# Full-attention layers in tiles of 64 rows by 32 columns, two banks for each sum, and a schedule by half steps

## The chip, the cores and the metric

The kernel runs on one core of a Trainium2 chip. The metric is device time in microseconds (us) for one execution. On this core TensorE (PE) does the matmuls, VectorE (DVE) and ScalarE (ACT) work on elements and read the matmul results, GpSimd (POOL) does a few element operations, and SyncE (SP) issues nearly all DMAs. Matmul results land in PSUM, of which the program uses eight banks of 128 partitions by 512 float32 columns.

## The reference

Four layers act on `x` of 2048 rows by 512 columns: `x = x + attention(layernorm(x))`, with weights A, B, A, B. Every attention has 32 heads of 16 columns:

```
qkv = x @ wqkv                       # 2048 x 1536 -> q, k, v per head
scores = q @ k.T * 16 ** -0.5
A only: scores outside 0 <= row - column < 256 are masked
p = softmax(scores)                  # over the keys
x = x + (p @ v) @ wo
```

Layers 0 and 2 (A) are windowed, layers 1 and 3 (B, "full") see all 2048 keys. The change is in the full layers.

## The kernel before

**Tiling.** A full layer goes over four blocks of 512 queries and eight groups of four heads ("quads"): 32 quads a layer, 64 in all. A quad takes 16 steps of 128 keys (`attn_full`). Scores are laid out with keys on the partitions. Float16 operands are split in high and low parts that lie in the 64 rows of each head, so a score matmul has 64 rows, 128 columns of weights (keys) and 512 queries, and two heads run in the two halves of the rows. One score tile (`s`, two banks) holds two heads, so a step has two tiles with two matmuls each (line 780). For each tile ACT computes one exponential of 128 x 1024 into a buffer `e` in SBUF (line 784; six buffers, `EB`).

**Values.** Two steps later (`flush(2)`), four float32 matmuls multiply the four heads' `e` with V (128 rows, 17 columns, the 17th a column of ones that gives the softmax denominator; line 895). Each has its own 32 columns of the array and its own 32 partitions of the bank `acc[0]`, where the 16 steps add up. The profile counts eight where the program has four, so a float32 matmul runs as two passes.

**Epilogue.** At the end of a quad DVE transposes `acc[0]` out of PSUM (line 739); the next quad's first value matmul must wait for that. Then DVE divides by the sums.

**The special step.** In most quads (58 of 64) step 4 (`JX`) is split in query halves instead of head pairs (`halves_of`). ACT takes one half (line 804). DVE takes the other (line 808) and computes its exponential by a polynomial of 16 operations (`chain`, lines 814 to 818), two after each step (`links`); its value matmuls (`part`, line 870) come at step 12 (`JV`).

**Side work.** Projections of this or the next layer run in the same PE stream: keys and queries (`project`), values (`values`), output (`wo`, `wo_part`). They are cut in tiles of 12 (or 3) products of 128 x 512 (or 128 x 256), each issued as four column tiles of 32 (line 402), in the bank `acc[1]`. One DVE operation, or two, then reads that bank. For keys and queries POOL squares the result, and a matmul with `hsum` (line 589) sums the squares per head ("squares"). Python generators hand out this work. `Side.share` gives each step what a budget allows, and `PH["free"]`, a clock kept at build time, holds the next tile back until the bank should be read. `Side.finish`, and two `while` loops that call `sd.one(True)`, issue what is left at given points without attention work between.

**Order.** PE's order is exactly the order in which the program issues (`manual_schedule`); the other engines are ordered by the scheduler. PSUM in a full layer: two banks for the two `acc`, four for two score tiles, two for a third score tile (`PH["third"]`).

## Time and profile before

| | |
|---|---|
| three runs | 2649.82, 2655.22, 2655.87 us; median 2655.22 |
| the profiled execution's own time | 2656.6 us |
| its span in the profile | 2654.8 us |
| granted PE clock | 0.996 of full speed |
| layer 0 and preparation | 0 to 446.36 us |
| layer 1 (full), first to last exponential | 446.36 to 1403.20 us |
| layer 2 (windowed) | 1403.20 to 1692.10 us |
| layer 3 (full) | 1692.10 to 2637.60 us |
| rest | 17.20 us |
| exponentials in the full layers | 1990, and 58 half steps on DVE |

The page gives PE 97% busy and ACT 88% over the span; in the two full layers ACT is busy 97%. A busy time is the union of the instructions' intervals. ACT's intervals overlap, so its busy share hides small waits, and the distance from one instruction to the next is the better reading. "PEld" are weight loads, which run beside the matmuls. "[idle before <- X]" names what an engine waited for.

### The profile page before, as it was taken

What the parts mean: (1) busy time and instruction counts of PE and PEld (TensorE: products, weight loads), DVE (VectorE), ACT (ScalarE), POOL (GpSimd) and SP (SyncE); (2) the same over time, 40 slices, a digit from 0 to 9 for tenths busy, and PEclk for the clock granted to TensorE, in tenths of its full rate; (3) what the DMA queues carried; (4) which work ended last, traced back from release to release, by engine and by line L of the source; (5) the groups of instructions that cost most, each with busy time, mean ns of one, the idle gap of its engine ahead of it and who ended that gap; (6) DMA issues with size and microseconds to landing.
All of it is one profiled execution on the core that took longest, in us unless ns stands there. A gap on an engine that the chain in (4) does not pass through costs nothing.

```text
span 2654.8 us, 65506 instructions
## 1 busy us (share of the span) xinstructions
PE 2581.0 (97%) x26897; PEld 798.5 (30%) x26897; DVE 1480.9 (56%) x2933; ACT 2342.9 (88%) x2667; POOL 588.4 (22%) x1215
## 2 busy tenths in 40 slices
PE   8999899999999999999999999999999999999998
PEld 3333344332222222222223444422222222222221
DVE  5746654446675566545416666455545553466554
ACT  5777665999999999999997787699999999999997
POOL 1889760000000000000006787000000000000000
PEclk9999999999999999999999999999999999999999
DMA  6878866133343234222425654423222234435441
GB/s 203 202 235 264 221 187 181 57 100 115 107 100 104 80 117 116 80 73 85 128 95 158 203 162 148 146 77 94 83 77 69 87 105 140 145 113 169 135 133 50
DMA packets 293199, 341.50 MB, mean 129 GB/s; under 512 B 105928, under 2 KB 199592, under 8 KB 288280
## 3 DMA queue, kind: packets, MB, share of 16 engines
q1 hardware_dynamic: 284376, 310.17, 39.0%
q0 software_dynamic: 8512, 27.04, 3.8%
q8 instruction: 213, 3.49, 0.6%
q14 instruction: 98, 0.80, 0.1%
HBM read 226.49 MB, written 96.99 MB: 122 GB/s over the span
## 4 chain that ended last, share of the span: by engine, by line
PE 85%; DVE 6%; ACT 5%; issue 2%; POOL 1%; DMA 1%; SPq 0%; ACTq 0%; DVEq 0%
PE acc L895 32%; PE s L780 21%; PE acc L402 11%; PE b L405 7%; PE acc L929 5%; ACT e L784 4%; PE b L402 3%; PE acc L870 2%; PE bs L405 2%; PE s L799 1%; DVE ch L818 1%; DVE ot L739 1%; DMA x<-in_A_x_dram 0%; DVE xh L469 0%; POOL e L921 0%
## 5 line engine op out<-in xcount | busy, mean ns | idle before, releaser
L784 ACT ACTIVATE e<-s 128x1024 f32<-128x1024 f32 (+1 forms) x2316 | 2150.9, 1065 | 150.0 <-PE s L780 133.9
L895 PE MATMUL acc<-e,vt 128*17 128x512 f32 x7728 | 1017.7, 598 | 3.8 <-DVE z L56 1.6
L780 PE MATMUL s<-qt,kt 64*128 64x512 f16 (+3 forms) x5216 | 715.2, 353 | 22.7 <-ACT e L784 13.1
L818 DVE SCALAR_TENSOR_TENSOR ch<-ch 128x512 f32<-128x512 f32 x580 | 404.8, 698 | 13.4
L780 PEld LDWEIGHTS <-kt 64*128 64x128 f16 x5216 | 185.0, 94 | 673.6 <-issue 652.3
L739 DVE STREAM_TRANSPOSE ot<-acc 128x512 f32<-128x512 f32 x128 | 91.4, 714 | 436.8 <-PE acc L895 333.9
L921 POOL TENSOR_SCALAR_AFFINE_SELECT e<-e 128x256 f32<-128x256 f32 x512 | 233.1, 463 | 65.4 <-ACT e L784 64.4
L895 PEld LDWEIGHTS acc<-e,vt 128*17 128x17 f32 x7728 | 134.6, 95 | 347.3 <-issue 304.8
L918 POOL TENSOR_SCALAR_AFFINE_SELECT e<-e 128x256 f32<-128x256 f32 x448 | 195.8, 444 | 42.2 <-ACT e L784 39.3
L929 PE MATMUL acc<-e,vt 128*17 128x384 f32 (+2 forms) x2816 | 195.8, 387 | 0.6 <-POOL e L918 0.5
L405 PE MATMUL b<-xc,w 128*128 128x512 f16 x520 | 124.6, 384 | 8.9 <-DMA xc<-xh 5.9
L808 DVE TENSOR_SCALAR ch<-s 128x1024 f32<-128x1024 f32 x58 | 71.0, 1224 | 90.9 <-PE s L799 83.0
L686 POOL TENSOR_SCALAR vt<-vt 128x16 f32<-128x16 f32 (+1 forms) x48 | 17.9, 373 | 465.9 <-DVE vt L681 458.0
L764 POOL TENSOR_TENSOR oh<-o,oh 128x512 f16<-128x512 f32 x19 | 22.1, 1163 | 444.4 <-DVE oh L763 385.3
L402 PE MATMUL acc<-wv,xc 128*32 128x256 f16 (+1 forms) x2304 | 117.2, 299 | 0.0
L402 PEld LDWEIGHTS <-xc 128*32 128x32 f16 x2688 | 76.8, 97 | 121.9 <-issue 113.5
L402 PE MATMUL acc<-xc,w 128*32 128x512 f16 x1344 | 108.5, 379 | 0.3 <-DVE m_None L618 0.3
L570 POOL TENSOR_TENSOR sq_h<-sp_h 128x512 bf16<-128x512 f16 x27 | 28.1, 1039 | 354.6 <-DVE sp_h L564 321.3
L402 PE MATMUL acc<-xc,w_h 128*32 128x512 f16 x1296 | 104.3, 379 | 1.1 <-DVE m L618 0.6
L570 POOL TENSOR_TENSOR sq<-sp 128x512 bf16<-128x512 f16 x28 | 29.1, 1040 | 342.5 <-DVE sp L564 325.3
L681 DVE COPY vt<-acc 128x256 f32<-128x256 f32 (+1 forms) x48 | 23.5, 490 | 132.3 <-PE acc L402 132.2
L405 PEld LDWEIGHTS <-w 128*128 128x128 f16 x656 | 60.1, 98 | 98.1 <-issue 34.4
(179 smaller groups left out, 2192.0 us busy)
## 6 DMA issues: line engine op xcount, KB each, us to landing
kt<-kf SPq DMA_DIRECT2D x126, 512.0 KB
xd<-x SPq DMA_DIRECT2D x96, 256.0 KB
qt<-qs SPq DMA_DIRECT2D x96, 256.0 KB
x<-xd SPq DMA_DIRECT2D x96, 256.0 KB
w<-wd SPq DMA_DIRECT2D x16, 1024.0 KB
qs<-sp SPq DMA_DIRECT2D x48, 256.0 KB
wv<-wd SPq DMA_DIRECT2D x20, 512.0 KB
x<-in_A_x_dram SPq DMA_DIRECT2D x32, 256.0 KB
```

The source lines that it names most:

```text
L402: nc.tensor.matmul(ps[g:g + 32], a[:, g:g + 32], b, start=(i == 0), stop=(i == len(pairs) - 1), skip_group_check=True)
L405: nc.tensor.matmul(ps, a, b, start=(go and i == 0), stop=(i == len(pairs) - 1))
L570: nc.gpsimd.tensor_tensor(sq, sp[:, 0], sp[:, 0], ALU.mult)
L739: nc.vector.transpose(ot.rearrange("p b r -> p (b r)"), a)
L780: nc.tensor.matmul(ps[:, h, s0:s0 + wd_], kt[R * h:R * h + R, pr, kc:kc + P], qt[R * h:R * h + R, pr, qc:qc + wd_], start=True, stop=True)
L784: LAST["ACT"] = nc.scalar.activation(e[:, :, w0:w1], ps[:, :, w0:w1], AF.Exp, scale=SCALE).ins
L808: LAST["DVE"] = nc.vector.tensor_scalar(e, ps, SCALE * LOG2E, X_MIN, op0=ALU.mult, op1=ALU.max).ins
L818: chain.append(lambda y=y, i=i, d=d: v.scalar_tensor_tensor(y, y if i else t, d, t if i < len(X_POLY) - 1 else r, op0=ALU.add, op1=ALU.mult))
L895: nc.tensor.matmul(a[32 * h:32 * h + DH + 1, :], V[l, qd // 4, j // 8][:, j % 8, 4 * (qd % 4) + h, :], es_[h // 2][:, h % 2, :], start=(j ...
L918: last = nc.gpsimd.affine_select(v, v, pattern=[[0, 2], [-1, P]], compare_op=ALU.is_gt, fill=0.0, base=0, channel_multiplier=1)
L921: last = nc.gpsimd.affine_select(v, v, pattern=[[0, 2], [1, P]], compare_op=ALU.is_ge, fill=0.0, base=0, channel_multiplier=-1)
L929: nc.tensor.matmul(a[32 * h:32 * h + DH + 1, q * P:(q + nb) * P], V[l, (4 * c + j) // 4][:, j % 4, 4 * qd + h, :], es_[h // 2][:, h % 2, s ...
```

## The change

All matmuls of the full layers become tiles of 64 rows by 32 columns; the sums and products stay the same.

- A score tile is written by eight matmuls (four groups of 32 keys, two heads) instead of two.
- A value matmul is cut in two row halves. Each half adds into its own bank: `acc[0]` holds keys 0 to 63 of all steps, `acc[1]` keys 64 to 127. The epilogue transposes both banks (lines 782 and 784 after the change) and adds them (786).
- A side product is cut in the same way into two new banks (`PH["side"]`, `sd0` and `sd1`). `joined` copies one bank to SBUF and adds the other (lines 401 and 402). For `wo` a second multiply-add takes the place of `joined`. The squares are also split and joined.
- To find the two banks, the third score tile goes: two score tiles are left, which alternate.
- The schedule goes by slots, one per score tile (two per step): the slot's scores, one unit of values (four heads, half of the 512 queries) of four slots before (`LAG`; five in the first slots of a quad), at most one side product (`Side.slot`), and one operation of the polynomial.
- The special step loses one quad (57 on DVE, 1991 exponentials on ACT).

```diff
-JX, JV = 4, 12
+JX, JV, LAG = 4, 12, 4
...
-        if PH["full"] or not PH["win"] and "pool" not in PH or l is None and PH.get("third"):
+        if PH["full"] or "pool" not in PH or l is None and PH["side"] is not None:
             ps_x.close()
-            PH["pool"] = ps_x.enter_context(tc.tile_pool(name=f"ps_x{l}", bufs=1 if PH["full"] else 2, space=bass.MemoryType.PSUM))
-            PH["third"] = PH["pool"].tile([P, 2, QC], F32, name=f"s{l}") if PH["full"] else None
+            opened = lambda name, bufs: ps_x.enter_context(tc.tile_pool(name=f"{name}{l}", bufs=bufs, space=bass.MemoryType.PSUM))
+            PH["scores"], PH["pool"] = opened("ps_s", 2), opened("ps_x", 1 if PH["full"] else 2)
+            PH["side"] = [PH["pool"].tile([P, QC], F32, name=f"sd{r}_{l}") for r in range(2)] if PH["full"] else None
...
-            return acc[1]
+            return PH["side"]
...
+    def split(ps, a, b, start, stop, t=None):
+
+        for g in range(0, P, 32) if t is None else (32 * t,):
+            for r in range(2):
+                c = slice(g, g + 32) if t is None else slice(0, 32)
+                nc.tensor.matmul(ps[r][g:g + 32, :b.shape[-1]], a[64 * r:64 * r + 64, c], b[64 * r:64 * r + 64],
+                                 start=start, stop=stop, skip_group_check=True)
+
+    def joined(ps, to):
+
+        with tc.high_priority(HEAD_START):
+            nc.vector.tensor_copy(to, ps[1])
+            LAST["DVE"] = nc.vector.tensor_tensor(to, ps[0], to, ALU.add).ins
+        return to
...
-        if PH["full"] and pend:
-            settle()
-            PH["free"] = clock[0] + 1.6
-            yield 0.1
+        if PH["full"]:
+            PH["unit"] = PH["now"]
+            if pend:
+                settle()
+                PH["free"] = clock[0] + 2.2
+                yield 0.25
+            for i, (a, b) in enumerate(pairs):
+                split(ps, a, b, i == 0, i == len(pairs) - 1)
+                spent(us)
+                if i < len(pairs) - 1:
+                    yield us
+            PH["free"], PH["unit"] = clock[0] + after + (0.6 if chain else 0.0), None
+            READ.append(0)
+            return
...
+            if PH["full"]:
+                ps = joined(ps, vp.tile([P, QC], F32, name=f"pj{n}_{t}", tag="xn", bufs=1))
...
+            if PH["full"]:
+                split(ph, hsum, sq, True, True, t)
+            else:
+                nc.tensor.matmul(ph[32 * t:32 * t + 32, :], hsum, sq, start=True, stop=True, skip_group_check=True)
+        if not PH["full"]:
+            return ph
+        r = slice(32 * min(sqs), 32 * max(sqs) + 32)
+        to = vp.tile([P, QC], F32, name=f"ps{n}", tag="oe")
+        joined([ps[r] for ps in ph], to[r])
+        return to
...
+                if PH["full"]:
+                    n0, n1 = (0, D) if h is None else (x * HH * DH, (x + 1) * HH * DH)
+                    joined([b[:, n0:n1].rearrange("p (h d) -> p h d", d=DH) for b in ps], to)
...
+                for b in ps if PH["full"] else (ps,):
+                    LAST["DVE"] = nc.vector.scalar_tensor_tensor(xs[i], b, 1.0 / (UP[2] * UP[3]), xs[i], op0=ALU.mult, op1=ALU.add).ins
...
+            if l % 2:
+                os = vp.tile([P, QC // 32, 32], F32, name=f"os{n}", tag="oe")
+                nc.vector.transpose(os.rearrange("p b r -> p (b r)"), acc[1])
+                a = acc[0]
             nc.vector.transpose(ot.rearrange("p b r -> p (b r)"), a)
+        if l % 2:
+            nc.vector.tensor_tensor(ot[:, :, :DH + 1], ot[:, :, :DH + 1], os[:, :, :DH + 1], ALU.add)
...
+    def scores(name, kt, qt, kc, pr=None, x=None):
+
+        ps = PH["scores"].tile([P, 2, QC], F32, name=f"s{name}", tag="s")
+        for p, n in ((0, slice(0, QC // 2)), (1, slice(QC // 2, QC))) if pr is None else ((pr, slice(0, QC)),):
+            m = slice(x * QC // 2, (x + 1) * QC // 2) if pr is None else n
+            for g in range(0, P, 32):
                 for h in range(2):
...
+                    nc.tensor.matmul(ps[g:g + 32, h, n], kt[R * h:R * h + R, p, kc + g:kc + g + 32], qt[R * h:R * h + R, p, m],
+                                     start=True, stop=True, skip_group_check=True)
+        spent(0.23)
+        if x == 1:
+            e = CH["tile"][:, 0:2]
+            with tc.high_priority(HEAD_START):
+                LAST["DVE"] = nc.vector.tensor_scalar(e, ps, SCALE * LOG2E, X_MIN, op0=ALU.mult, op1=ALU.max).ins
+            for h in range(2):
+                polynomial(e[:, h])
+            return e
+        e = pp.tile([P, 2, QC], F32, name=f"e{name}", tag="e", bufs=EB)
+        LAST["ACT"] = nc.scalar.activation(e, ps, AF.Exp, scale=SCALE).ins
+        return e
...
+    def attn_full(l, c, qd, kt, qt):
+
+        def unit(j, x, where):
+            def go():
+                for h in range(4):
+                    for r in range(2):
+                        e = where(h)[64 * r:64 * r + 64]
+                        o = acc[r][32 * h:32 * h + DH + 1, x * QC // 2:(x + 1) * QC // 2]
+                        nc.tensor.matmul(o, V[l, qd // 4, j // 8][64 * r:64 * r + 64, j % 8, 4 * (qd % 4) + h, :], e,
+                                         start=(j == 0 and x == 0), stop=(j == NT - 1), skip_group_check=True)
+                spent(0.43)
+            return go
+
+        special = CH["tile"] is not None
         for j in range(NT):
+            name, kc, es_ = f"{l}_{c}_{qd}_{j}", j % 8 * P, []
+            if special and j == JX:
+                for x in range(2):
+                    e = scores(f"{name}_{x}", kt[j // 8], qt, kc, x=x)
+                    u = unit(j, x, lambda h, e=e: e[:, h % 2, h // 2 * QC // 2:(h // 2 + 1) * QC // 2])
+                    if x:
+                        held[l, c, qd] = u
+                    yield None if x else u
                 continue
             for pr in range(2):
+                es_.append(scores(f"{name}_{pr}", kt[j // 8], qt, kc, pr))
+                yield unit(j, pr, lambda h, x=pr, es_=es_: es_[h // 2][:, h % 2, x * QC // 2:(x + 1) * QC // 2])
...
-        def share(self):
-
-            self.budget = min(self.budget + max((self.cost - self.spent) / max(self.steps - 3 - self.k, 1), self.least), 0.75)
-            self.lag = max(self.lag - max(0.29, self.least), -0.3) + PH["skew"]
-            PH["skew"] = 0.0
-            while self.q and clock[0] >= PH["free"] and self.budget >= MM / 2 and (self.lag < 0.25 or self.budget > 0.45):
+        def slot(self):
+
+            self.budget = min(self.budget + max((self.cost - self.spent) / max(self.steps - 3 - self.k, 1), self.least) / 2, 0.75)
+            n = 0
+            while self.q and n < 1 and clock[0] >= PH["free"] and self.budget >= MM / 2:
                 c = self.one()
                 if c is None:
                     break
                 self.budget -= abs(c)
-                self.lag += abs(c)
+                n += abs(c) > 0.05
...
+    def quad(l, t, c, qd, ops, sd):
+
+        special = CH["tile"] is not None
+        at = PH["slots"]
+        for n, new in enumerate(attn_full(l, c, qd, *ops)):
+            j, pr = divmod(n, 2)
+            if pr == 0:
+                if (l, t, c) == (3, 0, 0):
+                    sd.least = 0.28 if LOW.done else 0.5
+                    while sd.k == NT - 5 and not LOW.done:
+                        sd.one(True)
+                while (l, c, qd) == (1, 0, NQD // 2) and sd.k == NT - 5 and not LAST_UP.done:
+                    sd.one(True)
+                sd.step()
+            if new is not None:
+                fullq.append([at + n + LAG + (n < (2 * JX + 1 if special else 10)), new, None])
+            if n == 2 * NT - 1:
+                fullq[-1][2] = lambda: epilogue(l, c, qd, None)
+            if n == 2 * JV + LAG + 1 and (l, c, qd) in held:
+                assert not chain
+                fullq[0:0] = [[at + n, held.pop((l, c, qd)), None]]
+            clock[0] = max(clock[0], PH["began"] + 0.9)
+            PH["began"] = clock[0]
+            then, ends = [], []
+            while fullq and fullq[0][0] <= at + n:
+                _, f, end = fullq.pop(0)
+                then.append(f)
+                if end:
+                    ends.append(end)
+            for f in then:
+                f()
+            if len(then) < 2:
+                sd.slot()
+            for f in ends:
+                f()
+            links(1)
+        PH["slots"] += 2 * NT
```

Three places show how the instructions stand. In the names, `s1_1_2_3_0` is the score tile of layer 1, block 1, quad 2, step 3, first head pair; `e` the exponential of the same numbers; `oh` and `wo` operands of an output projection; a number of five digits only makes a name unique.

PE at the start of quad 2 of block 1 in layer 1, before: the two score tiles of step 2, the values of step 0 (which wait for DVE's transpose), a side product.

```order
L780 MATMUL s1_1_2_2_0_9718<-qt1_1_2_9295,kt1_1_2_0_9297 128x512 [waits Activation_49]
...
L780 MATMUL s1_1_2_2_1_9723<-qt1_1_2_9295,kt1_1_2_0_9297 128x512 [waits Activation_49]
...
L895 MATMUL acc0_81<-e1_1_2_0_0_9669,vt1_0_0_4382 17x512 [waits DVE_49]
...
L402 MATMUL acc1_82<-wo1_0_8974,oh1_0_3_7475 32x512
...
L780 MATMUL s1_5721<-qt1_1_2_9295,kt1_1_2_0_9297 128x512 [waits Activation_49]
...
L780 MATMUL s1_1_2_3_1_9744<-qt1_1_2_9295,kt1_1_2_0_9297 128x512 [waits Activation_49]
```

The same place after (slots 5 and 6 of the quad, and slots 8 to 11 with the special step; the first matmul of each group of eight or sixteen):

```order
L844 MATMUL s1_1_2_2_1_15140<-qt1_1_2_14130,kt1_1_2_0_14132 32x512 [waits Activation_49]
...
L921 MATMUL acc0_78<-e1_1_2_0_0_15014,vt1_0_0_4382 17x256 [waits DVE_49]
...
L395 MATMUL sd0_1_5725<-wo1_0_13385,oh1_0_3_9640 32x512
...
L844 MATMUL s1_1_2_3_0_15167<-qt1_1_2_14130,kt1_1_2_0_14132 32x512 [waits Activation_49]
...
L921 MATMUL acc0_78<-e1_1_2_0_0_15014,vt1_0_0_4382 17x256
...
L844 MATMUL s1_1_2_4_0_15213<-qt1_1_2_14130,kt1_1_2_0_14132 32x256 [waits Activation_49]
...
L844 MATMUL s1_1_2_4_1_15248<-qt1_1_2_14130,kt1_1_2_0_14132 32x256 [waits Activation_49]
...
L844 MATMUL s1_1_2_5_0_15283<-qt1_1_2_14130,kt1_1_2_0_14132 32x512 [waits Activation_49]
...
L844 MATMUL s1_1_2_5_1_15312<-qt1_1_2_14130,kt1_1_2_0_14132 32x512 [waits DVE_49]
```

A slot has one score tile, one unit of values and one side product; the unit in slot 6 is the last reader of `e1_1_2_0_0`. Of the two score tiles, slot 10 (`5_0`) takes the one that ACT read in slot 8 and slot 11 (`5_1`) the one that DVE reads.

DVE after one query projection of layer 3, before (two operations) and after (four):

```order
L564 TENSOR_SCALAR sp3_0_2_h0_0_24712<-acc1_82 128x512 [waits DMAHW4_49,DMAHW3_49,PE_49]
L565 SCALAR_TENSOR_TENSOR sp3_0_2_h0_0_24712<-acc1_82,sp3_0_2_h0_0_24712 128x512 [waits DVE_49]
```

```order
L401 COPY pj3_0_2_h0_0_43394<-sd1_3_39681 128x512 [waits PE_49]
L402 TENSOR_TENSOR pj3_0_2_h0_0_43394<-sd0_3_39680,pj3_0_2_h0_0_43394 128x512 [waits DVE_49]
L589 TENSOR_SCALAR sp3_0_2_h0_0_43397<-pj3_0_2_h0_0_43394 128x512 [waits DMAHW4_49,DMAHW3_49,DVE_49]
L590 SCALAR_TENSOR_TENSOR sp3_0_2_h0_0_43397<-pj3_0_2_h0_0_43394,sp3_0_2_h0_0_43397 128x512 [waits DVE_49]
```

The copy and the add stand ahead of the operation whose result POOL squares.

PE at the end of quad 1 of block 1 in layer 3, before: only the squares of one projection stand between the last values and the next quad's scores.

```order
L895 MATMUL acc0_81<-e3_1_1_13_1_24857,vt3_0_1_23206 17x512 x2
L589 LDWEIGHTS hsum_86 [waits DVE_49]
L589 MATMUL acc1_82<-sq3_1_1_h1_1_24899,hsum_86 32x512 [waits Pool_49]
L780 LDWEIGHTS kt3_2_0_0_24920 [waits DMAHW7_49,DMAHW0_49]
L780 MATMUL s3_2_0_0_0_24930<-qt3_2_0_24918,kt3_2_0_0_24920 128x512 [waits Activation_49]
```

After: five products of a query projection, its squares, all twelve products of a key projection and its squares stand there.

```order
L921 MATMUL acc1_79<-e3_1_1_13_1_43236,vt3_0_1_39601 17x256
L395 LDWEIGHTS w3_0_2_h0_42380
L395 MATMUL sd0_3_39680<-xc3_2_39083,w3_0_2_h0_42380 32x512
...
L395 MATMUL sd0_3_39680<-sq3_0_2_h0_0_43400,hsum_83 32x512 [waits Pool_49]
...
L395 LDWEIGHTS w3_1_1_h1_43154 [waits DMAHW2_49]
L395 MATMUL sd0_3_39680<-xc3_1_37609,w3_1_1_h1_43154 32x512 [waits DVE_49]
...
L395 MATMUL sd0_3_39680<-sq3_1_1_h1_1_43516,hsum_83 32x512 [waits Pool_49]
...
L844 LDWEIGHTS kt3_2_0_0_43528 [waits DMAHW0_49]
L844 MATMUL s3_2_0_0_0_43538<-qt3_2_0_43526,kt3_2_0_0_43528 32x512 [waits Activation_49]
```

`Side.finish` issues there what the slots had no room for.

123 lines of the change are left out of this document (38 added, 85 removed).

## The prediction

> **What bounds the kernel now.** I read the busy shares first, then the two full layers by stage, then PE's timeline in a step, then ACT's.
>
> ```profile
> PE 2581.0 (97%) x26897; PEld 798.5 (30%) x26897; DVE 1480.9 (56%) x2933; ACT 2342.9 (88%) x2667; POOL 588.4 (22%) x1215
> 446.36:1403.20 956.84, 945.58 (x9732) 241.85 (x9733) 514.25 (x949) 928.15 (x997) 55.92 (x70) 1.00 0.32 97
> 1692.10:2637.60 945.50, 935.06 (x9497) 244.49 (x9495) 504.15 (x893) 921.66 (x994) 53.73 (x62) 1.00 0.35 106
> ...
> 1289.54 1.05 PE L895 MATMUL acc<-e,vt 128*17 128x512 f32 x8
> 1290.41 0.61 PE L402 MATMUL acc<-wo,oh 128*32 128x512 f16 x8
> 1290.95 0.61 PE L780 MATMUL s<-qt,kt 64*128 64x512 f16 x4
> 1291.49 1.05 PE L895 MATMUL acc<-e,vt 128*17 128x512 f32 x8
> 1292.48 0.60 PE L780 MATMUL s<-qt,kt 64*128 64x512 f16 x4
> ...
> 1402.06 2.59 PE acc L402 x48
> ```
>
> The second and third rows are layers 1 and 3: length, then busy time (count) of PE, PEld, DVE, ACT and POOL. PE and ACT are both near full. A side product of four tiles takes 2.59/12 = 0.216 us (last row, from the chain of waits). From the starts: values 0.87 us, two side products 0.54 where two should take 0.43, scores 0.54 where two pairs should take 0.43, and values straight before scores 0.98. So each passage between the shapes 64x128 and 128x32 costs PE about 0.11 us, twice a step. A step with one side product takes 0.54 + 0.87 + 0.216 + 0.11 = 1.74 us, with two 1.95.
>
> ```profile
> 2444.08 27.61 ACT L784 ACTIVATE e<-s 128x1024 f32<-128x1024 f32 x30 [0.71 <-PE s L780]
> L784 ACT ACTIVATE e<-s x30: 1019/1186/1367, 2444.1 to 2470.3; 128x1024 f32<-128x1024 f32 x30
> ```
>
> Thirty exponentials without a wait: starts 26.2/29 = 0.904 us apart, but each lasts longer than the one before, 1.02 us at first and 1.37 at the end. Ends are therefore (27.61 - 1.02)/29 = 0.917 apart, and a score tile comes free at an end. I take 0.917 as ACT's pace, 1.83 a step: between PE's two step lengths. Over both full layers, 1902.3 us, the 1990 exponentials need 1990 x 0.917 = 1824; **ACT's ends lose only 78 us**. Whatever the change does for PE, it can win no more than this.
>
> **What PE wins.** Without changes of shape a step saves 2 x 0.11 us, 225 us over 1024 steps, all of it PE time. If eight half-height tiles run side by side as four do now, a slot (one score tile) needs 0.22 for scores, 0.44 for half a step's values and 0.216 for a side product: 0.87 us, under ACT's 0.917. No row shows eight tiles at once. The nearest are two row halves together (scores, four matmuls in 0.43) and four column groups together (side), so I take full overlap. [...] ACT then sets the pace of the full layers: 1991 x 0.917 = 1825 us plus what ACT loses. The sum is what it loses.
>
> **How much lateness ACT bears.**
>
> ```profile
> 446.36 2.83 ACT L784 ACTIVATE e<-s 128x1024 f32<-128x1024 f32 x3
> 447.41 0.39 PE L780 MATMUL s<-qt,ke 64*128 64x512 f16 x2 [0.78 <-ACT e L784]
> ...
> 2471.22 1.38 ACT L804 ACTIVATE e<-s 128x1024 f32<-128x1024 f32 x1
> 2471.32 1.23 DVE L808 TENSOR_SCALAR ch<-s 128x1024 f32<-128x1024 f32 x1 [1.54 <-PE s L799]
> 2472.01 0.40 PE L402 MATMUL acc<-xc,w_h 128*32 128x512 f16 x4
> 2472.34 0.70 PE L780 MATMUL s<-qt,kt 64*128 64x512 f16 x4
> 2472.84 3.01 ACT L784 ACTIVATE e<-s 128x1024 f32<-128x1024 f32 x3 [0.23 <-PE s L780]
> ```
>
> From ACT's end to PE's next score I take 0.05 us (446.36 + 1.02 to 447.41 is 0.03; from DVE to PE it is 0.05 in (c)); from the score to ACT's start 0.50 (2472.34 to 2472.84), 0.54 with six more starts (an estimate). With two alternating score tiles, exponential n+2 can start 0.05 + 0.54 = 0.59 after the end of n, and must start by 2 x 0.917 - 1.02 = 0.815. PE may be 0.225 us late; now, with a third tile, it may be a whole 0.917 later. Terms, each as ACT time lost:
>
> (a) *Special step, 57 x 0.69 = 39 us.* Slot 9's tile goes to DVE; slot 10 needs the tile ACT reads in slot 8. The next end is 0.05 + 0.54 + 1.02 = 1.61 after the last, 0.69 over pace. DVE's 1.23 us is over by then. Before, this step costs about as much, since PE is behind: at 2471 the end moves from 2472.60 to 2472.84 + 1.02, 0.34 over pace; at 1017 (next rows) from 1018.78 to 1019.62 + 1.02, 0.94. Bounds 35 (0.6 each) and 50 (DVE late).
>
> ```profile
> 1017.75 1.03 ACT L804 ACTIVATE e<-s 128x1024 f32<-128x1024 f32 x1
> 1019.62 2.85 ACT L784 ACTIVATE e<-s 128x1024 f32<-128x1024 f32 x3 [0.84 <-PE s L780]
> ```
>
> (b) *Six `e` buffers, 33 us.* At the start of a quad values run five slots late. Slots 6 and 8 (in the seven quads without special step 6 to 14, even) then write the `e` that the same slot's values still read. Those values end on PE 0.22 + 0.22 + 0.05 after the slot's score, plus 0.50: the exponential starts 0.99 after the score instead of 0.765, 0.22 lost. 57 x 2 + 7 x 5 = 149 times. Bounds 0 (if the buffers turn out a slot older) and 35.
>
> (c) *Epilogue, 19 us.*
>
> ```profile
> 1012.12 1.05 PE L895 MATMUL acc<-e,vt 128*17 128x512 f32 x8
> 1012.99 0.40 PE L402 MATMUL acc<-wo,oh 128*32 128x512 f16 x4
> 1013.24 0.72 DVE L739 STREAM_TRANSPOSE ot<-acc 128x512 f32<-128x512 f32 x1 [9.08 <-PE acc L895]
> 1013.88 0.65 DVE L704 SCALAR_TENSOR_TENSOR x<-acc,x 128x512 f32<-128x512 f32 x1
> 1014.01 0.62 PE L895 MATMUL acc<-e,vt 128*17 128x512 f32 x4
> ```
>
> DVE starts 0.25 after the values have streamed (1012.12 + 0.87 = 1012.99). Two transposes take 0.64 + 0.72, and PE resumes 0.05 later. The last values stand in slot 3, the first new ones in slot 5: from slot 3's score 0.67 + 0.25 + 1.36 + 0.05 = 2.33, wanted at 2 x 0.917 + 0.22 = 2.06. PE is 0.27 late, which slot 6 passes on through (b) unless slot 5 has no side product: 0.13 on average, and 0.17 more for a busy DVE. 62 x 0.3. Bounds 4 and 40.
>
> (d) *Forced runs, 37 us.* The slots take one product whatever its width, so half-width products are not finished in time. The order shows runs without scores: 42 half-width ones at the end of quad 3 and 29 in quad 4 of layer 1's first block, 31 in layer 3's first quad (12 there before), the place shown of layer 3's block 1, and two products with squares a block later.
>
> ```profile
> 1688.95 2.51 DMA qt<-qs
> 1713.37 1.31 PE acc L402 x48
> ...
> 1713.18 1.49 PE L402 MATMUL acc<-wv,xc 128*32 128x256 f16 x48
> 1714.72 0.42 DVE L681 COPY vt<-acc 128x256 f32<-128x256 f32 x1 [1.08 <-PE acc L402]
> ```
>
> A half-width product takes 1.31/12 = 0.11; the bank turns over in 0.23 (1714.49 to 1714.72) + 0.42 + 0.05, an add that I put at 0.45, + 0.05 = 1.2, once per twelve. 42: 4.6 + 3.6; 29: 3.2 + 2.4; 31: 3.4 + 2.4; each less 0.2: 19. The place shown: 17 x 0.216, twice 3.5 (next term) for squares, 1.7 for the bank (0.25 and two of 0.72), 2.5 for a `qt` that is only then loaded: 15. The last 4. Less 1.3 for the twelve before. Bounds 17 (PE's work alone) and 45.
>
> (e) *Squares, 18 us.*
>
> ```profile
> L570 POOL TENSOR_TENSOR sq_h<-sp_h 128x512 bf16<-128x512 f16 x27 | 28.1, 1039 | 354.6 <-DVE sp_h L564 321.3
> L564 DVE TENSOR_SCALAR sp_h<-acc x27: 651/692/693, 1731.4 to 2537.9; 128x512 f16<-128x512 f32 x27
> 2472.58 0.43 DVE L814 TENSOR_SCALAR ch<-ch 128x512 f32<-128x512 f32 x1
> ```
>
> From the last product: 0.42 to DVE, copy and add 0.72 each (0.69 and a gap), scaling from SBUF 0.49 (as L814), POOL 1.04, 0.1: 3.5 us, of which the copy and the add, 1.4, are new. In the order 24 squares stand three slots behind (2.75 us) and 24 four (3.67). The first wait 0.75, less 0.225, and 0.2 for a busy DVE. Behind a waiting square stand the next score and all of PE. Bounds 0 and 35.
>
> (f) *Other side tiles, 10 us, and layer ends, 1.* A `wo` bank turns over in 0.42 + 0.65 + 0.65 + 0.05 = 1.77, the next product comes two slots (1.83) on; only a busy DVE delays it. Bounds 0 and 25. DVE goes from 514 + 504 us busy in these layers to some 1290: 64 transposes and adds, 72 second multiply-adds, 137 joins of one or two operations.
>
> Sum: 1825 + 39 + 33 + 19 + 37 + 18 + 11 = 1982 for the full layers, against 1902.3: 79 us more. The windowed layers keep their work. The profiled execution took 2656.6, so 2735.6; it stands 1.4 over the median shown, and I forecast **2735 us**.
>
> **Rivals.**
>
> *PE's relief shows (faster).* If (b) vanishes, DVE is never late and the forced runs cost only PE's work, ACT loses 35 + 4 + 17 = 56 us instead of 78: 2634 us. For it: PE has 0.05 us to spare in each slot and 0.26 where no side product stands. Against it: with two tiles it may be 0.225 late and no more.
>
> *They cancel.* Losses of 70 to 86 us, 2648 to 2664.
>
> *Matmuls do not come fast enough (much slower).* A slot has 8 + 16 + 6 = 30 matmuls with 30 loads.
>
> ```profile
> 1632.00:1640.00 8.00, 7.69 (x175) 4.69 (x169) 7.48 (x22) 6.71 (x9) 6.25 (x16) 1.00 0.35 105
> ```
>
> The densest 8 us hold 175 matmuls, 46 ns each; 48 came in 1.31 us, 27 ns each. This decides from 0.917/30 = 30.6 ns. At 33 ns a slot lasts 0.99, the 2048 slots 2028, with (a), (d) and (e) 2122: 2876 us. Tiles that overlap only in part come to the same. [...]
>
> *DVE is the limit.* Sixteen polynomial operations and a projection's four fall in slots 9 to 25. If the polynomial is 1 us late at slot 29, PE waits there in 57 quads: 45 us more, 2780. Against: 1290 of 1982 us is 65%.
>
> **How the numbers follow.** Forecast 0.56, DVE limit 0.08, slow issue 0.07, cancel 0.08, faster 0.21. What can be told from no change is 0.3%, 8 us. Faster 0.21, same 0.08, slower 0.71. The low bounds of the terms together give 56 us, 2634; the high ones 230 us, 2808. The range is 2630 to 2810.
>
> **What would show it.** Right: ACT's idle time named PE; after the special slot 1.6 us between ends; exponentials of slots 6 and 8 waiting for values; the forced runs as gaps of 5 to 14 us; PE's changes of shape gone. Wrong: score groups of eight lasting over 0.25 us (then PE is the limit), or ends 0.917 apart through slots 6 and 8 and over a quad's start, with the full layers under 1900 us.

## The result and the profile after

The changed kernel takes 2902.89 us (median of four runs, 2890.60 to 2912.94), the kernel before 2653.38 in the same comparison: 1.094 times as long, 95% interval 1.089 to 1.099. The forecast was 2735 us, with a range up to 2810. The sign was right, the size was not: 79 us more were expected, 250 came. The profile shows the slowest of the four executions, 2912.94 us, so sums taken from it come out some 10 us over the median.

The page of the changed kernel, first the busy shares, then three groups of instructions (busy time, mean ns | idle time before them and what ended it), then the queue that brings the engines' instructions (packets, MB, share of the DMA engines):

```profile
PE 2612.4 (90%) x70272; PEld 1389.2 (48%) x70272; DVE 1724.5 (59%) x3342; ACT 2361.0 (81%) x2668; POOL 610.9 (21%) x1215
L855 ACT ACTIVATE e<-s 128x1024 f32<-128x1024 f32 x1991 | 1869.0, 1061 | 285.2 <-PE s L844 212.9
L595 POOL TENSOR_TENSOR sq_h<-sp_h 128x512 bf16<-128x512 f16 x27 | 39.2, 1453 | 512.9 <-DVE sp_h L589 400.1
q8 instruction: 551, 9.03, 1.3%
```

PE is at 90% where it was at 97, and ACT at 81 where it was at 88: neither is full any more. The exponentials wait 285 us, most of it for scores. The loss lies in the full layers (length, then PE, PEld, DVE, ACT, POOL busy, granted clock):

```profile
451.00:1499.00 1048.00, 949.36 (x31448) 537.11 (x31432) 617.50 (x1120) 932.31 (x998) 67.45 (x69) 0.98 0.31 91
1787.00:2894.00 1107.00, 961.64 (x31031) 538.47 (x31039) 642.76 (x1126) 937.09 (x996) 63.56 (x62) 0.97 0.31 93
```

From the first exponential to the last end they take 1047.7 and 1106.0 us, 2153.7 against 1902.3; the windowed layers changed by some 5. With the prediction's pace of 0.917 us, ACT's ends lose 134.6 + 193.8 = 328 us where 157 were expected, and lost 78 before. "Lost" is here and below the distance from one end to the next, less 0.917 us, added up.

What the change promised for PE came true. PE's timeline in the changed kernel (start, duration, tile, count):

```profile
2335.02 0.41 PE L844 MATMUL s<-qt,kt 64*32 64x512 f16 x8
2335.24 0.63 PE L921 MATMUL acc<-e,vt 64*17 64x256 f32 x16
2335.67 0.41 PE L395 MATMUL sd<-wo,ov 64*32 64x512 f16 x8
2335.88 0.41 PE L844 MATMUL s<-qt,kt 64*32 64x512 f16 x8
```

Scores to values 0.22, values to side 0.43, side to scores 0.21: eight small tiles run side by side, no passage between shapes costs anything, and a slot takes 0.86 us. But PE stands still between such slots. Its waits in the full layers of the changed kernel, down to 8.9 us (us in total, times, longest). In the first row PE is ahead and waits for ACT, which by itself costs ACT nothing:

```profile
PE s L844 <- ACT e L855: 34.7, 98, 1.0
PE sd L395 <- DVE x L763: 29.9, 29, 4.4
PE acc L921 <- issue: 28.8, 35, 2.3
PE sd L395 <- POOL sq_h L595: 28.4, 22, 3.6
PE acc L921 <- DVE ot L784: 24.6, 27, 6.2
PE sd L395 <- issue: 18.6, 19, 2.4
PE s L844 <- issue: 14.1, 19, 1.8
PE sd L395 <- DVE vt L402: 9.1, 9, 1.5
PE sd L395 <- DVE psk L402: 8.9, 7, 2.5
```

I put every late end of an exponential down to the largest cause of PE's stalls in the 2.6 us before it, and each stall to the instruction that ended some 0.1 us before PE went on; of slot 10's losses, 0.6 us each are put to the special step, so that row is in good part set by this rule. This sorting is worked out from the trace's records; no single row shows it, and where two stalls fall together it is a choice. ACT's lost time, both full layers, by cause:

| cause | ACT us lost | prediction's term |
|---|---|---|
| PE has no instructions ("issue") | 52 | none |
| second multiply-add of wo, L763 | 44 | (f): 10 with the joins |
| squares on POOL, L595 | 42 | (e): 18 |
| special step | 40 | (a): 39 |
| epilogue's transposes, L784 | 37 | (c): 19 |
| joins, L402 | 25 | in (f) |
| runs without scores, nothing else late | 24 | (d): 37 |
| PE at half clock | 23 | none |
| `e` buffers, nothing else late | 11 | (b): 33 |
| rest, most of it other DVE work | 30 | 1 |

### The profile page after: what moved, and what is told of

The parts are those of the page before. It is cut to its first block, busy times and chain, and to the rows that moved or that the text cites. A ratio compares the mean times of both kernels' runs of the same rounds, so it can differ in the third digit from the quotient of the medians.

```text
span 2910.9 us, 152756 instructions
## 1 busy us (share of the span) xinstructions
PE 2612.4 (90%) x70272; PEld 1389.2 (48%) x70272; DVE 1724.5 (59%) x3342; ACT 2361.0 (81%) x2668; POOL 610.9 (21%) x1215
## 4 chain that ended last, share of the span: by engine, by line
PE 54%; ACT 19%; DVE 16%; issue 8%; POOL 1%; DMA 1%; SPq 0%; ACTq 0%; DVEq 0%; POOLq 0%
PE acc L921 18%; ACT e L855 17%; PE s L844 11%; PE sd L395 7%; PE b L430 6%; PE acc L970 5%; PE b L427 3%; DVE ch L865 3%; PE s L826 3%; PE bs L430 2%; DVE ot L784 1%; DVE os L782 1%; DVE x L763 1%; ACT e L830 1%; DMA x<-in_A_x_dram 1%
## 5 line engine op out<-in xcount | busy, mean ns | idle before, releaser
L855 ACT ACTIVATE e<-s 128x1024 f32<-128x1024 f32 x1991 | 1869.0, 1061 | 285.2 <-PE s L844 212.9
L921 PE MATMUL acc<-e,vt 64*17 64x256 f32 x31856 | 1379.4, 383 | 57.4 <-issue 28.8
L844 PE MATMUL s<-qt,kt 64*32 64x512 f16 (+1 forms) x17008 | 949.8, 376 | 76.2 <-ACT e L855 30.0
L921 PEld LDWEIGHTS acc<-e,vt 64*17 64x17 f32 x31856 | 617.3, 94 | 243.4 <-issue 73.8
L844 PEld LDWEIGHTS <-kt 64*32 64x32 f16 x17008 | 408.7, 91 | 545.9 <-issue 410.8
L830 ACT ACTIVATE e<-s 128x1024 f32<-128x1024 f32 (+2 forms) x384 | 354.2, 970 | 100.2 <-PE s L826 85.7
L865 DVE SCALAR_TENSOR_TENSOR ch<-ch 128x512 f32<-128x512 f32 x570 | 405.8, 712 | 14.0
L395 PE MATMUL sd<-wv,xc 64*32 64x256 f16 (+1 forms) x4608 | 193.8, 301 | 16.5 <-DVE vt L402 9.1
L395 PE MATMUL sd<-xc,w_h 64*32 64x512 f16 x2592 | 157.6, 391 | 15.3 <-issue 6.1
L395 PE MATMUL sd<-xc,w 64*32 64x512 f16 x2688 | 156.3, 376 | 6.5 <-issue 6.3
L784 DVE STREAM_TRANSPOSE ot<-acc 128x512 f32<-128x512 f32 x128 | 88.8, 693 | 102.3 <-PE acc L970 102.3
L595 POOL TENSOR_TENSOR sq_h<-sp_h 128x512 bf16<-128x512 f16 x27 | 39.2, 1453 | 512.9 <-DVE sp_h L589 400.1
L763 DVE SCALAR_TENSOR_TENSOR x<-sd,x 128x512 f32<-128x512 f32 x120 | 82.6, 688 | 92.6 <-PE sd L395 86.9
L826 PE MATMUL s<-qt,kt 64*128 64x384 f16 (+2 forms) x1408 | 116.9, 275 | 16.6 <-ACT e L830 15.9
```

The source lines that it names most:

```text
L395: nc.tensor.matmul(ps[r][g:g + 32, :b.shape[-1]], a[64 * r:64 * r + 64, c], b[64 * r:64 * r + 64], start=start, stop=stop, skip_group_chec ...
L784: nc.vector.transpose(ot.rearrange("p b r -> p (b r)"), a)
L826: nc.tensor.matmul(ps[:, h, s0:s0 + wd_], kt[R * h:R * h + R, pr, kc:kc + P], qt[R * h:R * h + R, pr, qc:qc + wd_], start=True, stop=True)
L830: LAST["ACT"] = nc.scalar.activation(e[:, :, w0:w1], ps[:, :, w0:w1], AF.Exp, scale=SCALE).ins
L844: nc.tensor.matmul(ps[g:g + 32, h, n], kt[R * h:R * h + R, p, kc + g:kc + g + 32], qt[R * h:R * h + R, p, m], start=True, stop=True, skip_ ...
L855: LAST["ACT"] = nc.scalar.activation(e, ps, AF.Exp, scale=SCALE).ins
```

## Experiments

Three theories stood at the start. F (fetch): PE runs out of instructions. L (late DVE): DVE's work on the split banks stands behind other work. T (tiles): with two score tiles any lateness costs, and the third tile is what is missed.

### 1 to 3: does PE run out of instructions?

The "issue" rows are idle time in which PE waited for nothing that the profile shows. Before, they came to 0.7 us in all; now they come to 62. In PE's timeline of the changed kernel such a stall sits in the middle of one score group:

```profile
629.19 0.49 PE L395 MATMUL sd<-xc,w 64*32 64x512 f16 x8
629.47 0.39 PE L844 MATMUL s<-qt,kt 64*32 64x512 f16 x3
631.43 0.40 PE L844 MATMUL s<-qt,kt 64*32 64x512 f16 x5 [1.57 <-issue]
631.45 0.60 PE L395 MATMUL sd<-xc,w 64*32 64x512 f16 x8
```

The third and the fourth matmul belong to one group: they read and write the same tiles. The transfers of the instruction queue are 16,384 bytes each; 551 of them for PE's 140,724 records make 255 instructions per packet, and on average 256 are used between the starts of two. In the full layers more than 0.5 us pass 286 times between the start of one PE record and the next ("gaps" below). Of these gaps 66 (77 us) end 1.25 to 1.5 us after a packet has landed; in the kernel before, 4 of 270 do. If the 286 had nothing to do with packets, some 16 would fall there, an estimate from the mean spacing of packets, 4.42 us. Run 1 takes some four tenths of the full layers' transfers away (91 and 93 GB/s become 54 and 57):

```
 def load_full(l, c, qd):
+    if l not in ONCE:
+        ONCE[l] = load_first(l, c, qd)   # the old body
+    return ONCE[l]
...
-    matmul(pf[:1, :1], okay[:, 0:1], onesf)
+    matmul(pf[:1, :1], onesf, onesf)
```

> The changed kernel without the loads of K and Q in the full layers: each full layer loads the two K tiles and the Q tile of its first quad and uses them for all 32 quads, so the attention of the other quads is left out of the result; every matmul, exponential, DVE operation and instruction stays, and the flag of the range test is set. Theory F (fetch): PE runs out of instructions. One 16 KB packet of the instruction queue holds 256 of them, 128 matmuls with their loads; a slot now has 30 such pairs, so PE uses a packet in some 3.9 us (before: 12.8), and a packet that starts behind 0.5 to 2 MB of other transfers comes 1.5 to 4 us late. F expects the PE gaps over 0.5 us that end 1.25 to 1.5 us after a packet has landed (30 in layer 1 and 36 in layer 3, 41 and 36 us long together) to fall below 20, the half-speed windows of the clock from 27 to some 15, and the time from 2903 to 2790 to 2840 us. Theory L (late DVE: second reads of the split banks, joins and epilogue stand behind polynomial links) and theory T (the third score tile is missed) expect no change: 2890 to 2915.

2860.81 us, ratio 1.077 (1.074 to 1.079): 42 us less than the changed kernel. The gaps of that kind fell from 66 to 36 (38 us), and the rows of that run are:

```profile
PE s L844 <- issue: 10.2, 13, 2.7
PE acc L928 <- issue: 8.2, 11, 1.9
PE sd L395 <- issue: 4.2, 5, 1.3
```

23 us are left of 62. Fewer than 20 gaps and 2790 to 2840 us were expected, and neither came; the stretches at half clock stayed too, 23 in the full layers with the loads and without. So the mechanism is there, at about half the price expected. The control, with the same edit to the kernel before:

> The kernel before with the same loads left out in the same way (the attention of all but the first quad's K and Q is left out of the result). A packet of instructions lasts PE 12.8 us there, so F expects no change, 2645 to 2660 us; so do L and T. If it becomes faster by more than 10 us, the loads cost something by themselves, and the gain of the changed kernel without loads is not due to the instructions.

2653.14 us, ratio 0.9998 (0.9987 to 1.0008): the loads cost nothing where a packet lasts 12.8 us (median in the full layers of the kernel before: 12.82 and 13.01). Run 3 keeps the result and only makes the loads small:

```
-for v in range(len(kts), 2):
-    kt = pp.tile([P, 2, S // 2], F16, tag="kt", bufs=3)
+for v in range(len(kts), 8):
+    kt = pp.tile([P, 2, S // 8], F16, tag="kt", bufs=12)
```

> The changed kernel with K in eight pieces of 256 columns (128 KB) per quad and twelve buffers, in place of two of 1024 (512 KB) and three: the same bytes, but a piece is loaded when the piece before it in its buffer has been used, so that an instruction packet stands behind at most some 128 to 256 KB of K. F expects part of what leaving the loads out gives: 30 to 80 us, 2820 to 2873 us, and fewer than 35 of the gaps that end 1.25 to 1.5 us after a packet. L and T expect no change, 2890 to 2915.

2874.84 us, ratio 1.084 (1.081 to 1.086): 28 us less, just short of the bound named; 47 gaps (48 us) are left, more than 35. At 30 pairs of load and matmul in 0.917 us PE uses up a packet in 3.9 us (an estimate; in the full layers of the changed kernel the median from one packet's start to the next is 3.81 and 4.13), so there is little time for one that comes late: the packets ahead of the 66 gaps started 5.3 us after the one before (median; up to 8.7). The shortest time between two packets was 3.24 us; 128 pairs at 27 ns take about as long (3.45), so this is not shown to be a limit of the delivery. How far ahead packets are fetched no run settles.

### 4: what the third score tile was worth

```
-ps = PH["third"] if PH["full"] and turn["s"] % 3 == 0 else ps_s.tile(...)
+ps = ps_s.tile(...)
```

> The kernel before, with two score tiles of two banks in place of three and nothing else changed. T expects at least 100 us more than 2653: PE may be 0.225 us late with two tiles, and the values of a whole step, 0.87 us, stand between two score groups there. If PE's own work is what bounds the kernel before, whatever the number of tiles, it stays within 30 us of 2653, and the missing tile is not what the change lost.

2880.84 us, ratio 1.085 (1.083 to 1.088). One tile less, and the kernel before loses 227 us, about as much as the change lost. ACT's ends lose 303 us in place of 78: some 8 us per layer in most of the even slots, and 35 per layer in slot 10, behind the special step. The windows and the timeline of that run:

```profile
447.40:1517.80 1070.40, 991.66 (x9724) 270.83 (x9727) 514.53 (x949) 949.79 (x997) 55.89 (x70) 1.00 0.29 87
1806.30:2863.60 1057.30, 982.47 (x9499) 268.14 (x9498) 505.15 (x893) 949.25 (x994) 53.68 (x62) 1.00 0.31 94
...
1295.02 1.05 PE L895 MATMUL acc<-e,vt 128*17 128x512 f32 x8
1295.89 0.61 PE L402 MATMUL acc<-xc,w 128*32 128x512 f16 x8
1296.43 0.60 PE L780 MATMUL s<-qt,kt 64*128 64x512 f16 x4
1296.92 1.03 ACT L784 ACTIVATE e<-s 128x1024 f32<-128x1024 f32 x1 [0.46 <-PE s L780]
```

Values and side products, 1295.02 to 1296.43, stand between two score groups, 1.41 us. The third tile is what let ACT run on meanwhile; without it ACT waits 0.46 there. The change gives this tile up. At equal tiles the changed kernel is 22 us slower than this one, so the split of the tiles won nothing back as it stood; with the mends of run 11 below (2801 us) it is 80 us faster. The 227 us are the tile's price in the kernel before, where a whole step's values stand between score groups. In the changed kernel it is half a step's, and no run gave that kernel a third tile, so the price there is not measured.

### 5: is it the polynomial on DVE?

```
 nc.vector.tensor_scalar(e, ps, 0.0, 1.0, op0=ALU.mult, op1=ALU.max)
-for h in range(2):
-    polynomial(e[:, h])
```

> The changed kernel without the sixteen polynomial operations on DVE per special step; DVE still reads slot 9's score tile in one operation, but writes ones in place of the scaled scores, so half a step of each such quad is left out of the result, and the flag of the range test is set. PE's and ACT's instructions stay. DVE loses some 57 x 16 x 0.6 = 550 us of work. Theory L: PE's waits for DVE in the full layers (30 us for the second multiply-add of wo, 25 for the transposes, 22 for joins) fall by more than half, and with them half-speed windows; 2800 to 2850 us. Theories F (fetch) and T (two score tiles bear only 0.2 us of lateness, whatever the cause) without L expect at most 15 us: 2885 to 2905.

2860.78 us, ratio 1.076 (1.072 to 1.080): 42 us less, between the two theories. In layer 3 ACT's loss falls from 194 to 139 us: behind L763 from 44 to 12, behind the joins from 19 to 8. Squares and transposes stay (38 and 16). In layer 1 it rises from 135 to 143, since ACT's loss behind "issue" stalls grew from 28 to 45 there. So the polynomial holds up the multiply-adds of wo, in part the joins, and little else.

### 6 and 8: runs without scores, and later reuse of the side banks

```
-n += abs(c) > 0.05
+n += (abs(c) > 0.05) * (0.5 if abs(c) < 0.15 else 1)
```

> The changed kernel with up to two half-width side products per slot in place of one. The order then has no forced runs but one of 16 half-width products; in the changed kernel there are runs of 42, 29, 31 half-width and 17 whole products. By the prediction's term (d) the runs cost 37 us of ACT time; the ends of the exponentials behind them lose 43 us in the trace. Expected if (d) is right: 2860 to 2870 us against 2903. If the runs only move the work and the products cost the same elsewhere (a slot with two half-width products has no spare time more): 2890 to 2905.

2889.62 us, ratio 1.089 (1.086 to 1.092): 13 us less, which is not clear of the noise, as the four runs of the changed kernel alone span 22 us. At the five places the loss does go, in three of them nearly whole: 11.2, 5.3, 6.0, 16.0 and 4.1 us become 0.8, 0, 4.7, 3.4 and 0. But layer 1 as a whole went from 135 to 142 us, as ACT's loss behind "issue" stalls rose from 28 to 51; layer 3 lost 31 us less. The time lies just under the second range (2890 to 2905), far from the 2860 to 2870 expected if the term was right. So the term was about right at its places, and part of the gain went into another wait. Run 8 adds a slot before a bank is used again, also ahead of squares:

```
-PH["free"], PH["unit"] = clock[0] + after + ..., None
+PH["free"], PH["unit"] = clock[0] + after + 0.9 + ..., None
...
-    PH["free"] = clock[0] + 2.2           # ahead of squares
+    PH["free"] = clock[0] + 2.2 + 0.9
```

> The kernel of the run with two half-width products a slot, in which in addition a side bank is used again one slot (0.9 us) later than planned, and squares stand one slot later. Forced runs come back: about 70 whole products, 15 us of PE's work. Theory L: PE's waits in front of side products (30 us for the second multiply-add, 32 for the squares on POOL, 22 for joins) fall by more than half, and the half-speed windows with them; net 20 to 50 us below the run with two halves alone. Theories F and T without L: 10 to 20 us above it, by the forced runs.

2890.49 us, ratio 1.089 (1.087 to 1.091): no change, where L expected at least 20 us less. Two things lie behind this. The squares did profit: PE's waits for them fell from 17.4 us in run 6 to 12.8. But a wait for Q tiles came, which run 6 does not have and whose cause stays open:

```profile
PE s L844 <- DMA qt<-qs: 22.7, 5, 6.1
```

Behind L763, the reads that the edit was to relieve, PE still waits 27.1 us (26.1 in run 6) and ACT still loses 34. So these waits do not come from a reuse that is a slot too early. The timeline of the changed kernel, DVE and then PE at one such place, shows DVE's order:

```profile
2662.10 0.43 DVE L861 TENSOR_SCALAR ch<-ch 128x512 f32<-128x512 f32 x1
2662.56 0.69 DVE L862 SCALAR_TENSOR_TENSOR ch<-ch 128x512 f32<-128x512 f32 x1
2663.29 0.43 DVE L863 TENSOR_SCALAR ch<-ch 128x512 int32<-128x512 int32 x1
2663.63 2.86 DVE L865 SCALAR_TENSOR_TENSOR ch<-ch 128x512 f32<-128x512 f32 x4
2666.53 0.69 DVE L763 SCALAR_TENSOR_TENSOR x<-sd,x 128x512 f32<-128x512 f32 x1
2667.13 0.68 DVE L865 SCALAR_TENSOR_TENSOR ch<-ch 128x512 f32<-128x512 f32 x1
2667.73 0.68 DVE L763 SCALAR_TENSOR_TENSOR x<-sd,x 128x512 f32<-128x512 f32 x1
...
2667.27 0.58 PE L395 MATMUL sd<-wo,ov 64*32 64x512 f16 x1 [4.37 <-DVE x L763]
2668.47 0.62 PE L395 MATMUL sd<-wo,ov 64*32 64x512 f16 x7 [0.62 <-DVE x L763]
```

Seven links of the polynomial stand ahead of the first multiply-add, an eighth between the two. ACT's next exponential waited 5.81 us.

### 7: is it the width of the columns that makes a passage cost?

```
-for h in range(2):
-    nc.tensor.matmul(ps[:, h, ...], kt[R * h:R * h + R, pr, kc:kc + P], ...)
+for g in range(0, P, 32):
+    for h in range(2):
+        nc.tensor.matmul(ps[g:g + 32, h, ...], kt[R * h:R * h + R, pr, kc + g:kc + g + 32], ...)
```

> The kernel before, with three score tiles, values and side products in 128x32, and only the scores in eight tiles of 64 rows by 32 columns in place of two of 64 by 128. If the 0.11 us that PE loses at a passage between shapes is due to the change of the columns' width (128 to 32), the passages become free, PE wins up to 225 us of its own time and ACT up to its 78 us of lost time: 2590 to 2635 us. If it is due to the change of rows (64 to 128), nothing changes: 2645 to 2660. Instructions: 38 pairs per step, a packet per 6 us, so F expects few waits for instructions.

2672.51 us, ratio 1.0069 (1.0047 to 1.0091): 0.7% slower. PE's timeline of this run:

```profile
1290.71 1.05 PE L901 MATMUL acc<-e,vt 128*17 128x512 f32 x8
1291.58 0.61 PE L402 MATMUL acc<-wo,oh 128*32 128x512 f16 x8
1292.13 0.63 PE L785 MATMUL s<-qt,kt 64*32 64x512 f16 x16
1292.68 1.05 PE L901 MATMUL acc<-e,vt 128*17 128x512 f32 x8
```

0.87, 0.55, 0.55, as before, and no gain; that the time is even some 12 us over the 2645 to 2660 expected for that case stays unexplained. The shapes on both sides of a passage now have 32 columns, so the 0.11 us belong to the change of rows, 128 to 64 and back.

### 9 to 12: mending what was found, one by one

Each run adds one edit to the one before, from run 6 (2890) on. Theory A: the costs of late instructions add up. Theory B: a wait that is mended only lays another one bare.

```
+with tc.high_priority(HEAD_START):                            # 9
     for b in ps if PH["full"] else (ps,):
-        nc.vector.scalar_tensor_tensor(xs[i], b, ...)
+        LAST["DVE"] = nc.vector.scalar_tensor_tensor(xs[i], b, ...).ins
...
+bufs=12, K in pieces of S // 8                                # 10, as run 3
...
-... for a, b in TERMS], 2.2)                                  # 11
+... for a, b in TERMS], 3.1 if PH["full"] else 2.2)
...
-EB = 6, tag="qt" bufs=3, tag="sp" bufs=4                      # 12
+EB = 7, tag="qt" bufs=2, tag="sp" bufs=3
```

> The kernel with two half-width products a slot (2890 us); in addition DVE's two multiply-adds of a wo product in layer 3 are put ahead of the polynomial links that are ready at the same time (in the changed kernel up to five links of 0.7 us stand between or before them). Theory A (each late instruction costs PE its own stall, and the costs add): in layer 3 PE's stalls behind these multiply-adds, 39 us and 44 us of ACT time in the changed kernel, fall to about 12, as without the polynomial; 2850 to 2865 us. Theory B (with two score tiles any lateness costs, so one that is mended only lays another bare): less than half of it, 2870 to 2890.

2846.61 us (1.072, 1.069 to 1.075): 43 less, a little more than theory A expected. Behind the multiply-adds (now L764) ACT loses 6 us, and PE's row is:

```profile
PE sd L395 <- DVE x L764: 2.9, 7, 0.6
```

The changed kernel itself agrees. Layer 1's `wo` (line 744) has the same pair of multiply-adds, 24 in all, but with the priority that line 763 lacks, and no side product waits for one of them; for the 120 of line 763 PE waits 29 times. It is a partial control, since layer 1's tiles are longer, twelve products for three. The kernel before lacks the priority too (line 722), and with three score tiles and one read nothing in its trace waits for it.

> As the run before it, with K also in eight pieces per quad. Theory A: another 20 to 35 us less, as in the run with the eighths alone (28 us); theory B: less than 14.

2816.73 us (1.059, 1.057 to 1.062): 30 less, A.

> As the run before it, with the squares of a projection planned one slot (0.9 us) later. In the changed kernel PE's stalls behind the squares on POOL are 36 us long and cost ACT 42. Theory A: 20 to 35 us less than without; theory B: less than 10.

2800.65 us (1.054, 1.051 to 1.057): 16 less, between A and B. The squares' loss in ACT time went from 25 to 12.

> As the run before it, with seven buffers for exponentials in place of six (and for their memory two Q tiles in place of three and three buffers for split projections in place of four). Slots 6 and 8 then no longer write the buffer that the same slot's values read. Term (b) of the prediction puts this at 33 us; the ends at slots 6 and 8 lose 82 us in the changed kernel with everything that falls on them. Theory A: 25 to 40 us less than without; theory B, by which slot 6 loses what slots 4 and 5 were late by (epilogue) as soon as it does not wait itself: 5 to 20. All four mended by theory A: 2760 to 2790 us, near the 2735 that was forecast; the rest is the special step (40 us) and the epilogue.

2822.02 us (1.063, 1.060 to 1.066): 21 more, expected by neither. Slots 6 and 8 lose 24 us in place of 62, as A has it, but the full layers become only 9 us shorter (2041.1 after 2050.5): "issue" stalls rose by 16, slot 10 lost 11 more and other slots the rest, as B has it. Layer 1 starts at 472.0 in place of 445.3, which is more than the whole loss. This edit takes buffers from the layer ahead of it too; that they are the reason was not tested.

### 13 to 16: what is left

> Two half-width products a slot, wo's multiply-adds first and later squares, without the loads of K and Q after the first quad of a full layer (the attention of the other quads is left out of the result, the flag of the range test is set). To be held against the same mends with K in eighths, 2801 us. Theory F: what is left there of waits for instructions, 49 us of ACT time by the gaps that end 1.1 to 1.7 us after a packet, falls to some 20: 2765 to 2785 us. If the loads matter no more once K comes in eighths: 2793 to 2808.

With the edits of runs 6, 9 and 11 and that of run 1: 2786.63 us (1.050, 1.048 to 1.052), 14 below the 2801 with K in eighths, where 16 to 36 were expected. With the loads gone "issue" still costs ACT 41 us: other transfers, or PE catching up faster than packets come; which of them was not tried.

Run 14 undoes the halving of the values in the changed kernel:

```
-yield unit(j, pr, ...)
+yield unit(j, None, ...) if pr else None     # 512 columns
...
-LAG = 4
+LAG = 3
```

> The changed kernel with the values of a whole step in every second slot (512 columns, sixteen instructions pairs for a step in place of thirty-two), three slots after the step's second score. A step has 44 pairs in place of 60, a packet lasts 5.3 us. PE's work is the same, but it comes in pieces of 0.22, 0.86 and 0.22. Theory F alone: the waits for instructions, 52 us of ACT time, nearly vanish, 2840 to 2870 us. Theory T (two score tiles bear 0.225 us of lateness): the 0.86 us piece is 0.43 longer than half a step's, and behind it the next score comes late in every step that has a side product in that slot; 2950 to 3050 us.

2878.92 us (1.085, 1.083 to 1.087): 24 less, so neither. Its rows:

```profile
PE sd L395 <- issue: 4.2, 5, 2.1
PE acc L921 <- issue: 1.0, 1, 1.0
```

There are 431 packets in place of 551 and hardly a wait for them; but of the 52 us that these waits cost, more than half is lost again, by the sorting behind the longer piece. Run 16 has whole steps and all mends of run 11:

> The changed kernel with whole-step values (44 pairs of instructions per step), two half-width products a slot, wo's multiply-adds first, K in eighths and later squares. Theory A (the waits add by cause): 2801 us with half steps less most of the 49 us that waits for instructions still cost there, plus some 25 us for the longer piece of values: 2765 to 2785 us. Theory B (mended waits only lay others bare): 2795 to 2815. In either case it stays over 2653: the special steps (40 us) and the epilogues (34 us) are not mended.

2803.31 us (1.056, 1.054 to 1.058), theory B: within 3 us of the time with half steps, though its "issue" row is down to 1.6 us. In its place stand 68 us in 280 small losses behind no stall, only behind the ordinary longer pieces.

Run 15 undoes the split of the side products in the changed kernel:

```
-for r in range(2):
-    matmul(ps[r][g:g + 32], a[64 * r:64 * r + 64, c], b[64 * r:64 * r + 64], ...)
+matmul(ps[g:g + 32], a[:, c], b, ...)        # one bank, one read, no joins
```

> The changed kernel with side products and squares in four tiles of 128x32 and one bank, as before the change: one read by DVE, no joins, four pairs of instructions per product in place of eight; scores and values stay in 64x32. Theory P: each product brings two passages between shapes back, 0.22 us, a slot with a product lasts 0.22 + 0.43 + 0.22 + 0.22 = 1.09, over ACT's 0.917 in some 1150 of 2048 slots, up to 200 us more, less what the joins cost (some 110 us of ACT time behind second multiply-adds, joins and squares): 2950 to 3010 us. Theory J (the joins are what loses, and PE's free slots take the passages up): 2800 to 2870.

2937.10 us (1.108, 1.105 to 1.110): 34 more, nearest to P, a little below its range. Timeline of this run:

```profile
700.03 0.41 PE L834 MATMUL s<-qt,kt 64*32 64x512 f16 x8
700.25 0.61 PE L911 MATMUL acc<-e,vt 64*17 64x256 f32 x16
700.80 0.40 PE L394 MATMUL sd<-xc,w 128*32 128x512 f16 x4
701.13 0.41 PE L834 MATMUL s<-qt,kt 64*32 64x512 f16 x8
```

A slot with a side product lasts 1.10 us, by two passages of 0.11. No version with two score tiles came near the kernel before.

## Why the prediction was wrong

*What bounds the kernel, and PE's win: right.* ACT's pace, the 78 us that could be won, the full overlap of eight tiles, 0.87 us a slot (0.86) and the vanished passages are all in the traces. "Matmuls do not come fast enough" was wrong as it was put: 27 ns per pair (32 in the slot of 0.86 us above), not 33.

*How much lateness ACT bears: right in kind, and the heart of it.* 0.225 us with two tiles, 0.917 more with a third: no run measures the 0.225 by itself, but run 4 shows that the missing tile alone costs 227 us in the kernel before. The prediction used the number term by term, and never asked what it does to lateness that is not on its list.

*(a)* right: slot 10 loses 44 us for 39. *(d)* near in each place (11.2 us for 8.0, 5.3 for 5.4, 6.0 for 5.6, 16.0 for 15, 4.1 for 4); removing them gave 13 us, as part of it went into waits for instructions. *(b) and (c)* 82 us at slots 6 and 8 for 52. The buffers were put too high: 11 us by the sorting for 33, and run 12, which took 38 us away from these slots, made the layers only 9 us shorter. The transposes cost 37 for 19: in 11 of 64 quads DVE was still at other work and began up to 6 us late, some 18 us in all; in the others it began at once.

*(f), "only a busy DVE delays it": the failed step.* It was put at 10 us, at most 25, and cost 69 by the sorting. I took the bank's turnover as a chain of durations, 1.77 us against 1.83, and DVE's load as an average, 65%. What counts is DVE's order: up to eight links of the polynomial, 0.43 to 0.72 us each (2.86 for four L865), stand in front of or between the two multiply-adds. These cost 44 us and the joins 25, where 10 were expected for both. Runs 5 and 9 show it for the multiply-adds: 43 us by their order alone, and no side product waited for the pair with priority in layer 1. For the joins run 5 shows 11 us of it (19 to 8 in layer 3). The rival "DVE is the limit" had the right engine and the wrong place: slots 28 and 29, where I expected 45 us, lose 9.

*(e)* was mis-sized: 42 for 18. POOL's squares alone take 1.45 us where 1.04 was taken. The polynomial is not the reason, as they take 1.46 without it (run 5); the reason stays open.

*Missing in the sum, a second failed step: instructions.* The sum has no term for them, and the rival on issue asked only how fast matmuls can start, not how fast their code arrives. 3.2 times as many PE instructions in the full layers (62,479 matmuls for 19,229) make a packet last 3.9 us for 12.8, and K's loads then delay it (66 gaps, 36 without the loads of K and Q): 52 us of ACT time by the sorting; without the loads the kernel is 42 us faster (run 1), the kernel before not at all (run 2).

*Missing: the clock.* With PE's stalls came windows at half speed, 23 in the full layers for one before; they cost 23 us by the sorting. That the stalls bring them was not tested by a run of its own.

Of the 168 us over the forecast, instructions, DVE's order, squares and runs account for 102 by the mends (2903 to 2801). These include 13 that the forecast had counted in (d), so some 79 us of the 168 stay open. That distance is not settled piece by piece: in runs 6, 12 and 16 a mended wait partly uncovers another one, and that two tiles cannot absorb it is argued from the 0.225 us, not tested.

## What to carry to other kernels

When a change gives up a buffer between two engines that are both nearly full, price the buffer first, by taking it away alone; here it was worth 227 us in the kernel before, and the change's own win 78 at most. With less slack, waits that cost nothing before are paid for (run 4: ACT lost 303 us for 78), and an average load, forecast at 65% and measured at 58%, does not tell of them: read from the order what stands ahead of the instruction that is waited for. And count instructions: smaller tiles multiply them, and here a packet of them that PE uses up in 3.9 us brought a wait that one of 12.8 us did not.

## What the hardware showed beyond this

In the changed kernel PE's granted clock fell to 0.50 of full speed for 3.41 us, or a multiple, 27 times (the last, at the end of the run, lasted 7.73), each time after a stretch of that length in which PE had been idle for about half of the time or more. By the profile's busy time PE was busy for 0 to 42% of it before 23 of the 27 and for 45 to 51% before the other four. Six stretches at 44 to 50% kept the full clock, so no sharp bound comes out of this. The windows of the changed kernel around one stall (granted clock after the busy times):

```profile
2338.87:2342.28 3.41, 0.94 (x25) 0.49 (x32) 3.36 (x6) 0.53 (x1) 0.00 (x0) 1.00 0.27 77
2342.28:2345.69 3.41, 3.41 (x80) 1.79 (x64) 3.26 (x6) 2.05 (x2) 0.00 (x0) 0.51 0.32 106
2345.69:2349.10 3.41, 3.41 (x120) 1.84 (x112) 1.83 (x3) 3.37 (x4) 0.00 (x0) 0.99 1.03 324
```

The first holds 2.6 us of waiting for L763; in the second PE is busy throughout and runs 80 matmuls for 120 in the third. The 27 stretches come to 124 us; in the kernel before it was 5 with 24 us.
